# FFT and feed-forward on one core: the folds of w_in's second to fourth quarter from float32r halves

## The chip, the cores and the metric

The kernel runs on one core of a Trainium2 chip. The metric is the device time of one launch in microseconds (us). The kernel before takes 1676.99 us, the median of three runs (1676.96 to 1677.31).

A core has a matrix engine (TensorE, PE in the profile; its weight loads are PEld), VectorE (DVE), ScalarE (ACT), GpSimd (POOL) and SyncE (SP), which issues DMAs. Each engine takes its instructions in its own order and waits, where it must, for a count of another engine's finished instructions.

## The reference

`x` has 8 x 3008 rows of 256. A Fourier transform over both axes is taken and its real part kept; the result goes through a feed-forward layer of width 2048:

```
X = np.fft.fft(np.fft.fft(x, axis=1), axis=2).real     # (8, 3008, 256)
h = X.reshape(24064, 256) @ w_in                       # (24064, 2048)
g = np.where(h >= 1, h, np.where(h <= -1, 0, (h + 1) ** 2 / 4))
out = g @ w_out                                        # (24064, 256)
```

`w_in` and `w_out` come as float64 and are made float32 by the kernel itself.

## The kernel before

The transform over 256 columns is not taken for itself: its cosine and sine matrices (`mats`, two of 256 x 128, as four 128 x 128 tiles in `cm`) are multiplied into `w_in` once. This is the fold. It is done by quarters f4 of 512 columns, for the cosine (m = 0) and the sine (m = 1): fold n = 2 f4 + m, n = 0 to 7. A fold is two float32 matmuls into one PSUM bank `wps` (`fold_half`, one for each 128 rows of `w_in`). `fold_w_in` has ScalarE write the bank's high half to `wh`, rounded to float32r, and `fold_low` (s) has VectorE write what is left to `wl`. From fold 3, 5 and 7 ScalarE takes a row as well (R, `take_delta`), which four small DMAs (r, `move_delta`) spread to `delta`.

The main loop runs over units: 48 per batch element, one for each chunk of up to 512 columns and each block of 128 of the 2048. A unit i has on TensorE six float32r matmuls into two banks uv (`gemm1`: `wh` and `wl` with the high and low half of the transform), on VectorE a step us and two steps h, on ScalarE two steps a, on VectorE a step g, and on TensorE the acc matmuls (`gemm2`), some units later. The first 20 units take g as float32 and do four float32 acc matmuls; later ones take halves and do twelve in float32r. Three PSUM banks serve uv, and folds 3 and 5 take one of them as well. `SKIP` leaves units 7 and 11 without acc matmuls.

While the first units run, the weights are still being converted. Job n = 0, 1, 4, 5, 8, 9, 12, 13 is a half (128 rows) of a quarter of `w_in`, the others are parts of `w_out`. A conversion takes VectorE for two field steps (A, B or a), ScalarE (b), VectorE for one or two joins (c), and GpSimd for the products (d), whose result is `f32s[n]`, the tile `cv_n` in the profile. These tiles share a few buffers (tags h, a, gl), each of which goes round.

What runs when is written out by hand, in strings of one letter and a number per step: `START`, and for each unit `AHEAD` (between us and h on VectorE), `AMID` (after h), and `STEPS` (before `|`: ahead of the acc matmuls, after it: behind them). Up to unit 23 the engines' orders are pinned to the order of writing. Steps named `Q`, `W`, `M` and the like are put `behind_vector`: GpSimd starts them when VectorE's last instruction written before them is done.

In units 7 to 17 there lie the folds of quarters two to four: before, folds 2 and 3 between uv 7 and uv 8, folds 4 and 5 between uv 11 and uv 12, fold 6 behind the acc block of unit 15 and fold 7 before that of unit 17.

Of the kernel before, what the change touches and what calls it, by code (L numbers as in the profile page):

```python
# [9 lines left out]
F32 = mybir.dt.float32  # L10
F32R = mybir.dt.float32r
U32 = mybir.dt.uint32
I16 = mybir.dt.int16
AF = mybir.ActivationFunctionType
ALU = mybir.AluOpType
# [6 lines left out]
NB, S, D, FF = 8, 3008, 256, 2048  # L22
NA, NBB, NC = 64, 47, 24
P = 128
# [5 lines left out]
CH = 512  # L30
NCHUNK = 3
NFT = FF // P
ZPAD = 40
# [6 lines left out]
SHIFT = [23, 7, 7]  # L40
# [5 lines left out]
def _constants():  # L46
# [36 lines left out]
)  # L83
AHEAD = {1: "p12 v2 G0 q11", 2: "b3", 3: "p13 d3", 5: "L1", 6: "u1 d4", 7: "e14", 8: "M R1", 11: "d6", 12: "r2 M", 14: "s4", 15: "d7 e11", 17: "M u2", 18: "d10 M", 21: "M", 22: "u6 Q4", 23: "Q5", 30: "M M", 32: "M"}
AMID = {0: "p11 b2", 1: "h E1 q12", 4: "q13", 5: "p14", 6: "q14 A9", 7: "f2 B9 a8", 8: "b9 c8", 9: "c6", 11: "M a7 f4", 12: "b7", 16: "O1", 17: "a15 a14 f7", 18: "b14 b15", 19: "Q2 s7", 21: "c15", 22: "M", 25: "M M"}
STEPS = {
    0: "c2 | D1",
    1: "L0 e5",
# [2 lines left out]
    4: "b5 | L3 c4",  # L91
    5: "e6 | c5",
    6: "a12 d5",
    7: "b8 | b12 M s2 f3",
    8: "s3 d8 | a6 b6 e13",
    9: "r1 | c9 M",
    10: "u0 | d9 M L2",
    11: "f5 A13 R2",
    12: "c12 l11 B13 b13",
    13: "c13 d13 d12 | a10 s5",  # L100
    14: "e10 e7 b10 | c7",
    15: "M Q0 | f6 M",
    16: "s6 A11 B11",
    17: "R3 c10 | b11 e15 u3",
# [29 lines left out]
SPARE = (3, 5)  # L134
# [6 lines left out]
def fft_ffn_kernel(ctx: ExitStack, tc: tile.TileContext, x, xn, cst, w_in, w_out, out):  # L141
    nc = tc.nc

    wts = ctx.enter_context(tc.tile_pool(name="wts", bufs=1))
    sb = ctx.enter_context(tc.tile_pool(name="sb", bufs=1))
    dr = ctx.enter_context(tc.tile_pool(name="dr", bufs=1, space=bass.MemoryType.DRAM))
    ps = ctx.enter_context(tc.tile_pool(name="ps", bufs=1, space=bass.MemoryType.PSUM))
# [65 lines left out]
    cm = sb.tile([P, _OFF[6] - _OFF[2]], F32, tag="nyb", name="cm", bufs=4)  # L213
# [13 lines left out]
    def fft_bank(b, name):  # L227

        if name in BANK:
            return ps.tile([P, CH], F32, tag=BANK[name], name=name, bufs=1)  # L230
        if b == 0 and early[0] < EARLY_BANKS:
            early[0] += 1
            return ps.tile([P, CH], F32, tag=f"acc{early[0] % 4}", name=name, bufs=1)
        return ps.tile([P, CH], F32, tag="fft", name=name, bufs=1)
# [9 lines left out]
    raws, f32s, wo32, shared = {}, {}, {}, {}  # L244
# [95 lines left out]
    def behind_vector(ins):  # L340
        last = [ins for ins in traced if ins.engine == mybir.EngineType.DVE][-1]
        tc.add_manual_dep(ins, last.name, data_sync, reason="beside VectorE's next steps")

    folds, deltas, spreads = {}, {}, {}
# [21 lines left out]
    def fold_half(n, h):  # L366
        f4, m = divmod(n, 2)
        if h == 0:
            if f4 == 0 or n in SPARE:
                folds[n] = ps.tile([P, CH], F32, tag="uv", name=f"wps_{n}", bufs=3)  # L370
            else:
                folds[n] = fft_bank(f4, f"wps_{n}")
        nc.tensor.matmul(folds[n], mats[m][h], f32s[4 * f4 + h], start=(h == 0), stop=(h == 1))  # L373

    def fold_w_in(n):
        f4, m = divmod(n, 2)
        cols = slice(f4 * CH, (f4 + 1) * CH)
        if n not in folds:
            fold_half(n, 0)
        fold_half(n, 1)  # L380
        nc.scalar.activation(wh[m][:, cols], folds[n], AF.Copy, scale=inner if m else 1.0)

    def take_delta(f4):
# [14 lines left out]
    s1, s2, zn = {}, {}, {}  # L398
# [183 lines left out]
    def signs(i):  # L582
        return (slice(0, 1), slice(1, 2)) if i == n_units - 1 else (slice(0, 2),)

    def gemm1(i):
# [11 lines left out]
        nc.vector.scalar_tensor_tensor(us, nyb[b, k][:, :n], delta[:, f : f + 1], uv[0], op0=ALU.mult, op1=ALU.add)  # L597
        run_steps(AHEAD.get(i, ""))
        h = sb.tile([P, 2, CH], F32, tag="h", name=f"h_{i}", bufs=4)[:, :, :n]
# [3 lines left out]

        run_steps(AMID.get(i, ""))
        for sg in signs(i):
# [114 lines left out]
    def piece_sums(n):  # L720
# [31 lines left out]
        "v": lambda n: convert_scale(n, nc.vector),  # L752
        "F": lambda n: fold_half(n, 0),
        "f": fold_w_in,
        "G": activate,
        "s": fold_low,
        "u": w_out_high,
        "O": w_out_low,
        "Q": lambda n: behind_vector(w_out_low(n, nc.gpsimd)),
# [8 lines left out]
    def run_steps(names):  # L768
        for s in names.split():
            steps[s[0]](int(s[1:] or 0))  # L770
# [17 lines left out]
    for i in range(n_units + LAG):  # L788
# [29 lines left out]
        if i < n_units:  # L818
            run_steps(then)
            change = units[i][2] == (FIRST if b == 0 else 0) + LAG  # L820
            while pending and (change or units[i][2] != (FIRST if b == 0 else 0) + LAG - 1 and done < total * (r + 1 - r0) / (per - r0)):
                change = False
                w, f = pending.pop(0)
                f()
                done += w
                n = XC if b + 1 < PLAIN else XT
# [92 lines left out]
```

## Time and profile before

| | |
|---|---|
| median of three runs | 1676.99 us |
| the profiled execution | 1677.08 us |
| its span, first to last instruction | 1675.3 us |
| TensorE busy | 1669.6 us (100%) |
| VectorE, ScalarE, GpSimd busy | 81%, 79%, 71% of the span |
| granted TensorE clock | 1.000 |

A busy TensorE is one that has a matmul in flight: matmuls are pipelined, a record of 0.39 us stands for one that follows the last by 0.23 us, and a float32 matmul makes two records. The chain of waits gives TensorE's time without that overlap. Times of the rows are from the start of the span.

### The profile page before, as it was taken

To read this page: it belongs to the slowest core of one execution; us is meant where nothing else is said; L and a number is where in the kernel's file an instruction comes from. 1 tells how busy PE (TensorE), PEld (TensorE's weight loads), DVE (VectorE), ACT (ScalarE), POOL (GpSimd) and SP (SyncE) were. 2 spreads that over 40 slices of the span, in tenths; PEclk is the share of its full clock that TensorE was granted. 3 is DMA by queue.
4 is the path that set the end of the run, shared out by engine and by line. 5 is a ranking of instruction groups with operands and counts; after the bars stand their busy time and mean duration, and the time that the engine had idled before them with its cause. 6 is when DMAs were issued, how large, how long until landed. Compare 5 with 4: busy or idle time off the path is not lost.

```text
span 1675.3 us, 21422 instructions
## 1 busy us (share of the span) xinstructions
PE 1669.6 (100%) x7722; PEld 1382.0 (82%) x7722; DVE 1364.4 (81%) x1743; ACT 1327.8 (79%) x1527; POOL 1185.7 (71%) x957
## 2 busy tenths in 40 slices
PE   9999999999999999999999999999999999999999
PEld 6557888888888888888888888888888888888887
DVE  8998899877887787877887778787787777788776
ACT  6778878877888777887788877888778887778786
POOL 2447869856987568976789657896588866566664
PEclk9999999999999999999999999999999999999999
DMA  9113111100011000110010100101001010000000
GB/s 351 49 51 117 57 63 58 62 14 32 26 45 62 20 26 26 57 49 20 26 59 24 54 15 26 63 20 62 18 15 63 1 37 32 1 26 22 3 25 26
DMA packets 35705, 75.49 MB, mean 45 GB/s; under 512 B 4624, under 2 KB 13840, under 8 KB 35600
## 3 DMA queue, kind: packets, MB, share of 16 engines
q1 hardware_dynamic: 35420, 74.00, 12.5%
q8 instruction: 60, 0.98, 0.2%
q14 instruction: 45, 0.37, 0.1%
q10 hardware_dynamic: 180, 0.14, 0.0%
HBM read 46.31 MB, written 27.81 MB: 44 GB/s over the span
## 4 chain that ended last, share of the span: by engine, by line
PE 99%; DVE 1%; DMA 0%; issue 0%; SPq 0%; ACT 0%; DVEq 0%
PE acc L680 62%; PE uv L594 30%; PE s L549 2%; PE s L419 2%; PE wps L373 1%; PE s L424 0%; DMA raw<-in_moe_w_in_dram 0%; DVE us L597 0%; DVE h L600 0%; DVE h L601 0%; PE ny L523 0%; DVE g L620 0%; DVE pql L238 0%; DVE cv L304 0%; DVE cv L303 0%
## 5 line engine op out<-in xcount | busy, mean ns | idle before, releaser
L643 POOL TENSOR_TENSOR gl<-h,gh 128x512 fp32r<-128x512 f32 (+1 forms) x724 | 911.0, 1281 | 379.0 <-PE acc L680 207.4
L606 ACT ACTIVATE a<-h,biases 128x1024 f32<-128x1024 f32 (+1 forms) x385 | 436.0, 1133 | 242.5 <-DVE h L601 240.4
L680 PE MATMUL acc<-gh,woh 128*128 128x512 f32 (+1 forms) x1456 | 566.9, 389 | 0.0
L680 PE MATMUL acc<-gh,wol 128*128 128x512 f32 (+1 forms) x1456 | 558.8, 384 | 0.0
L680 PE MATMUL acc<-gl,woh 128*128 128x512 f32 (+1 forms) x1456 | 558.3, 383 | 0.0
L624 DVE SCALAR_TENSOR_TENSOR h<-a,h 128x1024 f32<-128x1024 f32 (+1 forms) x365 | 492.0, 1348 | 2.3 <-ACT a L607 1.0
L597 DVE SCALAR_TENSOR_TENSOR us<-nyb,delta,uv 128x512 f32<-128x512 f32 (+1 forms) x384 | 282.4, 735 | 243.8 <-PE uv L594 243.3
L627 ACT ACTIVATE gh<-h 128x1024 fp32r<-128x1024 f32 (+1 forms) x365 | 380.8, 1043 | 52.4 <-DVE h L624 38.1
L607 ACT ACTIVATE a<-a 128x1024 f32<-128x1024 f32 (+1 forms) x385 | 394.9, 1026 | 1.1
L680 PEld LDWEIGHTS acc<-gl,woh 128*128 128x128 f32 x1456 | 272.5, 187 | 52.0
L680 PEld LDWEIGHTS acc<-gh,woh 128*128 128x128 f32 x1456 | 273.0, 187 | 48.7
L680 PEld LDWEIGHTS acc<-gh,wol 128*128 128x128 f32 x1456 | 272.8, 187 | 48.6 <-DVE wol L335 0.3
L594 PE MATMUL uv<-pqh,wh 128*128 128x512 f32 (+1 forms) x768 | 303.2, 395 | 0.0
L600 DVE TENSOR_TENSOR h<-us,uv 128x512 f32<-128x512 f32 (+1 forms) x384 | 260.0, 677 | 51.1 <-POOL gl L643 0.8
L594 PE MATMUL uv<-pqh,wl 128*128 128x512 f32 (+1 forms) x768 | 294.3, 383 | 0.0
L594 PE MATMUL uv<-pql,wh 128*128 128x512 f32 (+1 forms) x768 | 294.3, 383 | 0.0
L601 DVE TENSOR_TENSOR h<-us,uv 128x512 f32<-128x512 f32 (+1 forms) x384 | 257.2, 670 | 0.0
L594 PEld LDWEIGHTS uv<-pqh,wh 128*128 128x128 f32 x768 | 143.8, 187 | 31.2 <-issue 3.8
L594 PEld LDWEIGHTS uv<-pqh,wl 128*128 128x128 f32 x768 | 143.7, 187 | 31.1 <-issue 5.0
L594 PEld LDWEIGHTS uv<-pql,wh 128*128 128x128 f32 x768 | 143.7, 187 | 27.6 <-DVE pql L238 0.4
L184 POOL TENSOR_TENSOR x<-x 120x256 f32<-120x256 f32 x84 | 96.5, 1149 | 13.7 <-DVE h L624 6.1
L189 POOL TENSOR_TENSOR x<-x 120x256 f32<-120x256 f32 (+1 forms) x49 | 65.7, 1341 | 11.1 <-DVE h L624 7.0
(85 smaller groups left out, 804.9 us busy)
## 6 DMA issues: line engine op xcount, KB each, us to landing
x<-in_xn_dram SPq DMA_DIRECT2D x42, 512.0 KB, 3.4
out_dram<-o SPq DMA_DIRECT2D x26, 512.0 KB, 2.7
out_dram<-o SPq DMA_DIRECT2D x14, 482.0 KB, 2.8
nyb<-nyr SPq DMA_DIRECT2D x24, 256.0 KB, 3.3
x<-in_x_dram SPq DMA_DIRECT2D x8, 512.0 KB, 7.3
raw<-in_moe_w_in_dram SPq DMA_DIRECT2D x4, 512.0 KB
raw<-in_moe_w_out_dram SPq DMA_DIRECT2D x4, 512.0 KB, 9.2
part<-o SPq DMA_DIRECT2D x4, 512.0 KB
```

The lines of the kernel that those rows point to most:

```text
L184: return nc.gpsimd.tensor_tensor(t[:, r], t[:, r], t[:, r + 1], op=ALU.add).ins
L189: return nc.gpsimd.tensor_tensor(t[:, 1], t[:, 0], t[:, 2], op=ALU.add).ins
L594: nc.tensor.matmul(t[:, :n], w[m][:, cols], r[:, m], start=(j == 0), stop=(j == 2))
L597: nc.vector.scalar_tensor_tensor(us, nyb[b, k][:, :n], delta[:, f : f + 1], uv[0], op0=ALU.mult, op1=ALU.add)
L600: nc.vector.tensor_tensor(h[:, 0], us, uv[1], op=ALU.subtract)
L601: last_h = nc.vector.tensor_tensor(h[:, 1], us, uv[1], op=ALU.add).ins
L606: nc.scalar.activation(a[:, sg], h[:, sg], AF.Relu, bias=half, scale=0.5)
L607: nc.scalar.activation(a[:, sg], a[:, sg], AF.Square)
L624: g = nc.vector.scalar_tensor_tensor(h[:, sg], a[:, sg], 1.0, h[:, sg], op0=ALU.min, op1=ALU.max).ins
L627: nc.scalar.activation(gh[:, sg], h[:, sg], AF.Copy)
L643: ins = nc.gpsimd.tensor_tensor(gl[:, sg], h[:, sg], gh[:, sg].bitcast(F32), op=ALU.subtract).ins
L680: nc.tensor.matmul(acc[:, :n], w, g[:, sg], start=(begin and j == 0), stop=(last and j == len(terms) - 1))
```

## The change

The folds of the second to fourth quarter (n = 2 to 7) take float32r. One new step S (`halve_mats`) has ScalarE copy the four matrix tiles to float32r (`hi`, 128 x 512) and GpSimd subtract that from them (`lo`). For each half quarter a step H (`halve_high`) has ScalarE copy `f32s[n]` to float32r and a step W (`halve_low`) has GpSimd subtract. All go to one tile `halved`, in the buffer of z, with room for one quarter. The fold is then six matmuls: high with high, matrix low with weight high, matrix high with weight low, each for two blocks of 128 rows. The two folds of the first quarter stay.

The strings move folds 2, 3, 4 and 5 behind the acc matmuls of units 8, 9, 12 and 13, with their low halves, rows and delta DMAs after them.

```
-AHEAD = {... 7: "e14", 8: "M R1", 11: "d6", 12: "r2 M", 14: "s4", ...}
+AHEAD = {... 7: "e14 S", 8: "M", 11: "d6", 12: "M", ...}
-AMID = {... 7: "f2 B9 a8", ... 11: "M a7 f4", ...}
+AMID = {... 7: "B9 a8", ... 11: "M a7", ...}
-    7: "b8 | b12 M s2 f3",
-    8: "s3 d8 | a6 b6 e13",
-    9: "r1 | c9 M",
-    10: "u0 | d9 M L2",
-    11: "f5 A13 R2",
-    12: "c12 l11 B13 b13",
-    13: "c13 d13 d12 | a10 s5",
-    14: "e10 e7 b10 | c7",
+    7: "H4 H5 W4 W5 b8 | b12 M",
+    8: "d8 | f2 a6 b6 e13",
+    9: "s2 | f3 R1 c9 M",
+    10: "s3 u0 | r1 d9 H8 W8 M L2",
+    11: "H9 W9 A13",
+    12: "c12 l11 f4 B13 b13",
+    13: "c13 d13 d12 s4 | f5 R2 a10",
+    14: "s5 H12 H13 W12 W13 e10 e7 b10 | r2 c7",
...
+        nc.scalar.activation(hi, cm, AF.Copy)
+        nc.gpsimd.tensor_tensor(lo, cm, hi.bitcast(F32), op=ALU.subtract)
+
+    def halve_high(n):
+        nc.scalar.activation(halved["w", 0, n % 2], f32s[n], AF.Copy)
+
+    def halve_low(n):
+        hi, lo = (halved["w", i, n % 2] for i in range(2))
+        behind_vector(nc.gpsimd.tensor_tensor(lo, f32s[n], hi.bitcast(F32), op=ALU.subtract).ins)
+
+    def fold_in_halves(n):
+        f4, m = divmod(n, 2)
+        if n in SPARE:
+            folds[n] = ps.tile([P, CH], F32, tag="uv", name=f"wps_{n}", bufs=3)
+        else:
+            folds[n] = fft_bank(f4, f"wps_{n}")
+        terms = [(i, j, h) for i, j in ((0, 0), (1, 0), (0, 1)) for h in range(2)]
+        for at, (i, j, h) in enumerate(terms):
+            w = halved["m", i][:, (2 * m + h) * P : (2 * m + h + 1) * P]
+            nc.tensor.matmul(folds[n], w, halved["w", j, h], start=(at == 0), stop=(at == len(terms) - 1))
```

On TensorE, before, behind unit 7's last uv matmuls (`uv_1_531`) and up to unit 8's (`uv_0_565`):

```order
L594 MATMUL uv_1_531<-pql_1_298,wh_69 128x512
L373 MATMUL wps_542<-cv_410,cm 128x512
L373 MATMUL wps_542<-cv_415,cm 128x512
L373 MATMUL wps_561<-cv_410,cm 128x512
L373 MATMUL wps_561<-cv_415,cm 128x512
L594 MATMUL uv_0_565<-pqh_2_389,wh_68 128x512
```

and now, from the same place to the fold, behind unit 8's uv (`uv_0_563`, `uv_1_567`) and an acc block:

```order
L629 MATMUL uv_1_531<-pql_1_298,wh_69 128x512
L629 MATMUL uv_0_563<-pqh_2_389,wh_68 128x512
...
L629 MATMUL uv_1_567<-pql_2_390,wh_69 128x512
L715 MATMUL acc_0_514<-g_512,wo_330 128x512
L715 MATMUL acc_1_515<-g_512,wo_330 128x512
L715 MATMUL acc_2_516<-g_512,wo_330 128x512
L715 MATMUL acc_3_517<-g_512,wo_330 128x512
L405 MATMUL wps_592<-halved 128x512 x6
```

The uv matmuls of units 7 and 8 now follow each other, and the fold stands one unit later.

On ScalarE now, between unit 10's last eviction and unit 12's first step (`a_702` is unit 11, `a_729` unit 12, `cv_546` and `cv_508` are the halves of the third quarter, n = 8 and 9):

```order
L731 ACTIVATE o_1_670<-acc_3_517 128x512
L390 ACTIVATE halved<-cv_546 128x512
L641 ACTIVATE a_702<-h_699,biases 128x1024
L642 ACTIVATE a_702<-a_702 128x1024
L390 ACTIVATE halved<-cv_508 128x512
L289 ACTIVATE cv_704<-cv_704 128x512
L290 ACTIVATE cv_704<-cv_704,biases 128x512
L292 ACTIVATE raw_wol<-raw_wol 128x512
L641 ACTIVATE a_729<-h_726,biases 128x2x482
```

Before, fold 4's eviction stood where the first copy to `halved` stands, and nothing where the second does.

On GpSimd now, from the product of `cv_508` to the second subtraction of that quarter (x are steps of the next batch element's input, `wo_697` a part of `w_out`):

```order
L320 TENSOR_TENSOR cv_508<-cv_508 128x512
L394 TENSOR_TENSOR halved<-cv_546,halved 128x512
L184 TENSOR_TENSOR x_1_458<-x_1_458 120x256
L320 TENSOR_TENSOR wo_697<-cv_600 128x512
L189 TENSOR_TENSOR x_1_458<-x_1_458 120x256
L394 TENSOR_TENSOR halved<-cv_508,halved 128x512
```

The three steps between stood there before as well; the subtractions are new ahead of them and behind them.

## Rows read from the trace of the kernel before

**Rows 1.** The page's engines: busy us (share of the span) x instructions.

```profile
PE 1669.6 (100%) x7722; PEld 1382.0 (82%) x7722; DVE 1364.4 (81%) x1743; ACT 1327.8 (79%) x1527; POOL 1185.7 (71%) x957
```

**Rows 2.** TensorE's waits, whole run: us in total, times, longest us.

```profile
PE warm_bank L713 <- POOL warm L708: 1.3, 1, 1.3
PE wps L373 <- DVE cv L320: 0.3, 1, 0.3
```

**Rows 3.** One stretch: us, busy PE, PEld, DVE, ACT, POOL; clock, DMA share, GB/s.

```profile
44.00:120.00 76.00, 76.00 (x234) 43.16 (x233) 74.09 (x109) 59.44 (x78) 33.23 (x32) 1.00 0.16 55
```

**Rows 4.** The chain of waits, 40 to 130 us: start us, us, what.

```profile
55.80 3.43 PE wps L373 x8
...
60.60 3.43 PE acc L680 x8
...
83.14 1.29 PE uv L594 x6
...
97.31 1.72 PE wps L373 x4
```

**Rows 5.** Timeline of VectorE: start us, us, engine, line, what.

```profile
55.85 0.73 DVE L597 SCALAR_TENSOR_TENSOR us<-nyb,delta,uv 128x512 f32<-128x512 f32 x1
...
60.04 0.71 DVE L396 TENSOR_TENSOR wl<-wps,wh 128x512 fp32r<-128x512 f32 x1
60.64 0.76 DVE L597 SCALAR_TENSOR_TENSOR us<-nyb,delta,uv 128x512 f32<-128x512 f32 x1
...
72.42 0.74 DVE L597 SCALAR_TENSOR_TENSOR us<-nyb,delta,uv 128x512 f32<-128x512 f32 x1
...
80.00 0.43 DVE L271 TENSOR_SCALAR cv<-raw 128x512 uint32<-128x512 uint32 x1
80.34 0.72 DVE L597 SCALAR_TENSOR_TENSOR us<-nyb,delta,uv 128x482 f32<-128x482 f32 x1
...
89.58 1.49 DVE L276 TENSOR_SCALAR cv<-raw 128x512 uint32<-128x512 uint32 x1
...
91.66 0.70 DVE L597 SCALAR_TENSOR_TENSOR us<-nyb,delta,uv 128x482 f32<-128x482 f32 x1
```

**Rows 6.** Timeline of ScalarE.

```profile
60.19 0.62 ACT L289 ACTIVATE cv<-cv 128x512 f32<-128x512 uint32 x1
...
74.59 1.15 ACT L606 ACTIVATE a<-h,biases 128x1024 f32<-128x1024 f32 x1 [3.35 <-DVE h L601]
...
76.73 0.61 ACT L331 ACTIVATE woh<-wo 128x512 fp32r<-128x512 f32 x1
...
79.64 1.18 ACT L606 ACTIVATE a<-h,biases 128x1024 f32<-128x1024 f32 x1
...
81.81 0.67 ACT L381 ACTIVATE wh<-wps,biases 128x512 fp32r<-128x512 f32 x1
```

**Rows 7.** GpSimd's groups, 44 to 120 us: busy us, mean ns, idle before.

```profile
L320 POOL TENSOR_TENSOR wo<-cv 128x512 f32<-128x512 f32 x4 | 5.1, 1286 | 8.8 <-DVE cv L304 4.5 <-ACT cv L289 4.2
L184 POOL TENSOR_TENSOR x<-x 120x256 f32<-120x256 f32 x5 | 3.7, 737 | 6.6 <-DVE cv L304 5.2 <-DVE g L620 1.4
...
L335 POOL TENSOR_TENSOR wol<-wo,woh 128x512 fp32r<-128x512 f32 x2 | 2.6, 1284 | 0.0
```

**Rows 8.** Timelines of VectorE and GpSimd where they meet.

```profile
97.28 1.59 POOL L297 TENSOR_SCALAR raw<-raw 128x512 f32<-128x512 uint32 x1
97.64 1.30 DVE L620 SCALAR_TENSOR_TENSOR g<-a,h 128x964 f32<-128x964 f32 x1
...
112.39 1.28 POOL L311 TENSOR_TENSOR cv<-cv,raw 128x512 f32<-128x512 f32 x1
112.46 2.23 DVE L620 SCALAR_TENSOR_TENSOR g<-a,h 128x964 f32<-128x964 f32 x1
```

**Rows 9.** SyncE's timeline, quarter two's delta DMAs; their line's time to landing.

```profile
63.31 2.46 SPq L362 DMA_DIRECT2D delta<-row  x4
DMA to landing us min/median/max: 2.0/2.0/2.8
```

More of the change, by code (lines that the diff above doesn't have):

```diff
@@ L83 @@
 )
-AHEAD = {1: "p12 v2 G0 q11", 2: "b3", 3: "p13 d3", 5: "L1", 6: "u1 d4", 7: "e14", 8: "M R1", 11: "d6", 12: "r2 M", 14: "s4", 15: "d7 e11", 17: "M u2", 18: "d10 M", 21: "M", 22: "u6 Q4", 23: "Q5", 30: "M M", 32: "M"}
-AMID = {0: "p11 b2", 1: "h E1 q12", 4: "q13", 5: "p14", 6: "q14 A9", 7: "f2 B9 a8", 8: "b9 c8", 9: "c6", 11: "M a7 f4", 12: "b7", 16: "O1", 17: "a15 a14 f7", 18: "b14 b15", 19: "Q2 s7", 21: "c15", 22: "M", 25: "M M"}
+AHEAD = {1: "p12 v2 G0 q11", 2: "b3", 3: "p13 d3", 5: "L1", 6: "u1 d4", 7: "e14 S", 8: "M", 11: "d6", 12: "M", 15: "d7 e11", 17: "M u2", 18: "d10 M", 21: "M", 22: "u6 Q4", 23: "Q5", 30: "M M", 32: "M"}
+AMID = {0: "p11 b2", 1: "h E1 q12", 4: "q13", 5: "p14", 6: "q14 A9", 7: "B9 a8", 8: "b9 c8", 9: "c6", 11: "M a7", 12: "b7", 16: "O1", 17: "a15 a14 f7", 18: "b14 b15", 19: "Q2 s7", 21: "c15", 22: "M", 25: "M M"}
 STEPS = {
@@ L373, in fold_half, with halve_mats @@
         nc.tensor.matmul(folds[n], mats[m][h], f32s[4 * f4 + h], start=(h == 0), stop=(h == 1))
+    halved = {}
+    def halve_mats():
+        t = sb.tile([P, ZPAD + NC * (P + 1)], F32R, tag="z", name="halved", bufs=1)
+        wide = 4 * P
+        for i in range(2):
+            halved["m", i] = t[:, i * wide : (i + 1) * wide]
+            for h in range(2):
+                o = 2 * wide + SHIFT[1] + (2 * i + h) * CH
+                halved["w", i, h] = t[:, o : o + CH]
+        hi, lo = (halved["m", i] for i in range(2))
+        nc.scalar.activation(hi, cm, AF.Copy)
[15 more added lines that the diff above has]
+            nc.tensor.matmul(folds[n], w, halved["w", j, h], start=(at == 0), stop=(at == len(terms) - 1))
     def fold_w_in(n):
@@ L377, in fold_w_in @@
         cols = slice(f4 * CH, (f4 + 1) * CH)
-        if n not in folds:
-            fold_half(n, 0)
-        fold_half(n, 1)
+        if f4:
+            fold_in_halves(n)
+        else:
+            if n not in folds:
+                fold_half(n, 0)
+            fold_half(n, 1)
         nc.scalar.activation(wh[m][:, cols], folds[n], AF.Copy, scale=inner if m else 1.0)
@@ L756, in fft_ffn_kernel @@
         "s": fold_low,
+        "S": lambda n: halve_mats(),
+        "H": halve_high,
+        "W": halve_low,
         "u": w_out_high,
```

## The prediction

> **What bounds the kernel now.** I read the page's table of engines first, then TensorE's waits, then the stage in which the change lies. TensorE is busy for 1669.6 of 1675.3 us [rows 1], and over the whole run its records show two waits, 1.6 us together, both in the first 9 us [rows 2]. Whatever is taken from TensorE, or makes it wait, therefore reaches the end one to one. The chain of waits in the stage from 40 to 130 us says the same: it runs through TensorE alone, units of six uv matmuls (1.37 us, the gap between the end of the fold block at 59.23 and the acc block at 60.60) and of four acc matmuls (3.43 us) [rows 4].
>
> But that stage has a second limit. From 44 to 120 us VectorE is busy for 74.1 of 76 us [rows 3]: it converts the weights beside its share of each unit. Its first step of unit 10 starts at 72.42 us [rows 5], 2.9 us after TensorE had the data (60.60 + 3.43 + 1.37 + 3.43 + 0.68 = 69.5 [rows 4]). TensorE does not notice, since a PSUM bank of uv is wanted again only one unit later. So the reader is to see a stage with TensorE full and VectorE full, the second a few us behind the first, and every queue in its written order. A wait put in front of VectorE here can't be made up before about 100 us.
>
> **The change part by part.**
>
> *The folds on TensorE.* Before, the second and third quarter's folds are two blocks of 3.43 us and the fourth quarter's two of 1.72 us [rows 4]: 10.3 us. A fold in halves is six float32r matmuls of 512 columns, which is what one unit's uv matmuls are: 1.37 us, six folds 8.2 us. Gain 2.1 us. [...]
>
> *Unit 8 directly behind unit 7.* The folds leave the place between uv 7 and uv 8, which has no acc block either. The second half of uv 8 takes the bank of uv 7's first, so it needs VectorE's us step of unit 7, 55.85 to 56.58 [rows 5]; TensorE is ready for it at 55.80 + 0.68 = 56.48. With 0.2 us for signal and start (an estimate, used below too): 0.3 us lost.
>
> *Fold 2's halves.* ScalarE reaches the two copies of `cv_4`, `cv_5` when unit 7's square is through, at 60.19, where its next instruction started before [rows 6]; a copy takes 0.61 us. GpSimd then subtracts twice, 1.28 us each [rows 7]: 60.85 to 63.4. TensorE wants the last of its six matmuls at 55.80 + 0.3 + 1.37 + 3.43 + 1.14 = 62.0, so it waits 1.6 us, or 2.2 if VectorE's two joins of `cv_8`, due in those us, get between the subtractions. This wait is not in the sum by itself: a later one, below, sets TensorE's time anew.
>
> *VectorE from unit 8 to 10.* The two low halves of quarter two (0.60 us each, from 60.04 to 60.64 [rows 5]) move: one out from before unit 8, one in before unit 10. Unit 8's step then starts at 60.04, unit 10's 72.42 - 60.64 = 11.78 us later, at 71.8. What is new there are GpSimd's subtractions of 1.28 us, beside VectorE's work. The rows show that some pairs don't run together: a field step of VectorE took 1.49 us instead of 0.43, started 0.1 us into a GpSimd instruction [rows 5], and a g step 2.23 beside GpSimd's add at 112.39 [rows 8]. So the two subtractions cost VectorE between 0 and 2 x 1.28 = 2.6 us. I take 1.6: one hit in full and a smaller one. [...]
>
> *The chain to fold 4 — the term that decides.* Let T be the start of ScalarE's first step of unit 10. It follows unit 10's us step by 74.59 - 72.42 = 2.17 us [rows 5, 6]: T is 74.0 without new hits, 75.6 with 1.6 us of them, 76.6 at most. From T, ScalarE does unit 10's two steps, woh, four evictions and one more copy before unit 11's first step, 79.64 - 74.59 = 5.05 us; the copy of `cv_8` (H8) takes the slot of the fold's eviction there. H8 is done at T + 5.2. Unit 11's two steps take 81.81 - 79.64 = 2.17 us, and only then stands the copy of `cv_9` (H9), done at T + 7.8. GpSimd has between its subtractions W8 and W9 two x steps (0.74) and a wo product (1.29) [rows 7]: W8 from T + 5.2 to 6.5, the three to T + 9.2, W9 to T + 10.5. GpSimd, not H9, is last.
>
> Two things wait for W9. Fold 4's sixth matmul does: TensorE starts uv 13 at T + 10.5 + 0.2 + 0.2 = T + 10.9 = 86.5, where before it started at 83.14 with fold 5 already done [rows 4]. And VectorE does: the first field step of `cv_13` (A13) takes the buffer of `cv_9`, whose last reader was fold 5 on TensorE and is now W9. It was at 80.00, directly before unit 12's us step at 80.34 [rows 5]; now it starts at T + 10.6 and unit 12 at T + 10.9 = 86.5, so VectorE, full until then, stands some 5 us. Behind it wait units 12 and 13 and the conversion of quarter four.
>
> *Behind that.* TensorE: uv 13 with 0.25 for its second bank, acc, fold 5 (1.37), uv 14 (1.29), acc: T + 22.0. VectorE needs 91.66 - 80.34 = 11.3 us from unit 12's to unit 14's us step [rows 5], with one low half (0.6) in either order, and 1.07 us of a hit inside. Until fold 5's low half is taken only two uv banks go round, so uv 15's first half waits for unit 14's us step, done at T + 23.0, and its second for unit 14's last h step, 2.1 us after the us step began, T + 24.4. The second half of uv 15 starts at T + 24.6 = 100.2. Before: 97.31 - 3.43 - 0.65 = 93.2 [rows 4]. TensorE is 6.9 us late. Folds 6 and 7 give back 0.35 each, fold 6 waits about 0.2 for its second subtraction.
>
> *The rest.* The four small delta DMAs of quarter two now stand on SP behind two part stores, which wait for the four evictions (T + 4.6): at 0.6 us an issue (2.46/4) the first is issued about T + 5.8 = 81.4 and landed 2.0 later [rows 9], 83.4. Unit 12 needs it at 86.5, so the A13 wait covers it; without that wait it would be what is late next, 3 us against the old 80.34. The tile of the halves uses z's buffer, wanted again only in unit 24: nothing. The extra 7 copies (0.61) and 7 subtractions (1.28) fit, ScalarE and GpSimd being busy for 59 and 33 of the 76 us [rows 3]; their places cost, not their sum. After 120 us nothing is done that would let TensorE catch up.
>
> **Sum.** 6.9 - 0.7 + 0.2 = 6.4 us later. The profiled execution took 1677.08 us, 1.8 around its span, and the median is 1676.99, the same within the runs' spread; 1677.0 + 6.4 = 1683.4.
>
> **Rivals.**
> 1. No new hits: T is 74.0 and the hit of 1.07 falls away, uv 15's second half at 97.5, +4.3 - 0.5: 1680.8. For it: GpSimd's subtractions are told to stand behind a VectorE step, whose next ones read PSUM. Against: the joins of `cv_8` come inside 2.6 us.
> 2. More hits: T = 76.6 and another 1.28 between units 12 and 14: +9.3 - 0.5, 1685.8. [...]
> 3. The other side: W9 is done before TensorE wants it, all halves are hidden, the 2.1 us remain: 1674.9. TensorE without waits wants fold 4's last matmul at 80.5 (six uv or folds of 1.37, four acc blocks, 1.29, 1.14 and 0.3 behind 55.80), so it decides whether T + 10.5 is below that: T would have to be 70.0, 4 us before its lowest value. Only a shorter way of ScalarE and GpSimd than the rows have would give it.
> 4. [...]
> 5. The change doesn't do what it says: six float32r matmuls, each with a new weight load, take no less than the float32 fold. +2.1 on the forecast: 1685.5. Against: the uv matmuls change weights each time too.
>
> **How the numbers follow.** Forecast 0.50, rivals 0.18, 0.18, 0.07, 0.04, 0.03. I take 0.2% (3.35 us) as what a measurement of this kernel tells from no change: slower is above 1680.35, faster below 1673.65. The forecast, rivals 2, 4, 5 and 0.10 of rival 1 lie above: 0.85. The rest of 1 and most of 3: 0.13. No case reaches faster; 0.02 for what I don't see. The range from 1679.9 to 1686.5 holds all but rivals 3 and 4 and the tails.
>
> **What the profile of the changed kernel would show.** The fold's rows as float32r, six of about 0.23 us each. A wait of 1.5 to 2.2 us on TensorE in fold 2, on GpSimd's halves; one of 1 us or more in fold 4, the same; VectorE idle for about 5 us before a field step near 86 us, released by GpSimd; uv 13 at 85 to 87.5 us; from 120 us on the same picture as before, 4 to 9 us later. If uv 13 starts before 83.5, or VectorE's pause isn't there, the chain to W9 is wrong; if uv 13 is right and uv 16 isn't 6 us late, the hits are mis-sized.

## The result and the profile after

The changed kernel takes 1686.11 us (median of 6 runs, 1685.51 to 1687.2), the kernel before 1676.97 (6 runs, 1676.86 to 1677.31): a ratio of 1.0055, with a 95% interval of 1.0044 to 1.0065. It is 9.1 us slower. The forecast was 1683.4, 6.4 us slower, with a range of 1679.9 to 1686.5: the direction and the place are right, the size is 2.7 us too small.

The page's engines come first, beside [rows 1]: TensorE has two more us of work in its records and GpSimd 12 more; the span is 9.0 us longer, 1684.3 instead of 1675.3.

```profile
PE 1671.7 (99%) x7734; PEld 1383.0 (82%) x7734; DVE 1369.3 (81%) x1743; ACT 1332.1 (79%) x1534; POOL 1198.1 (71%) x964
```

Then TensorE's waits over the whole run (us in total, times, longest us), where [rows 2] had two:

```profile
PE wps L405 <- POOL halved L394: 2.8, 2, 1.5
PE uv L629 <- DVE us L632: 1.9, 3, 1.5
...
PE uv L629 <- DVE h L636: 0.8, 2, 0.4
PE uv L629 <- DVE wl L429: 0.8, 1, 0.8
PE wps L405 <- ACT halved L390: 0.7, 1, 0.7
```

All of them lie between 56 and 103 us. TensorE now waits for GpSimd's halves in the folds, and for VectorE in the uv blocks. VectorE has two waits of its own between 44 and 130 us:

```profile
DVE cv L271 <- POOL halved L394: 5.0, 1, 5.0
DVE cv L303 <- POOL cv L287: 1.8, 1, 1.8
```

The first is the pause before A13, as forecast. The second, a join of `cv_6` that waits for GpSimd, was not in the forecast. The stretch of [rows 3] again shows both engines with holes, where both were full:

```profile
44.00:120.00 76.00, 68.89 (x218) 38.93 (x217) 67.78 (x96) 54.20 (x74) 38.69 (x33) 1.00 0.15 55
```

VectorE's timeline, beside [rows 5] (start us, us, engine, line, what; in brackets the idle time before it and its releaser):

```profile
62.47 1.75 DVE L304 SCALAR_TENSOR_TENSOR cv<-raw_wol,cv 128x512 uint32<-128x512 uint32 x1
64.15 1.63 DVE L655 SCALAR_TENSOR_TENSOR g<-a,h 128x1024 f32<-128x1024 f32 x1
...
70.47 0.69 DVE L303 SCALAR_TENSOR_TENSOR cv<-raw_wol,cv 128x512 f32<-128x512 uint32 x1 [1.85 <-POOL cv L287]
...
74.62 0.74 DVE L632 SCALAR_TENSOR_TENSOR us<-nyb,delta,uv 128x512 f32<-128x512 f32 x1
...
87.42 0.43 DVE L271 TENSOR_SCALAR cv<-raw 128x512 uint32<-128x512 uint32 x1 [5.01 <-POOL halved L394]
87.76 0.71 DVE L632 SCALAR_TENSOR_TENSOR us<-nyb,delta,uv 128x482 f32<-128x482 f32 x1
...
97.23 1.19 DVE L271 TENSOR_SCALAR cv<-raw 128x512 uint32<-128x512 uint32 x1
98.34 1.49 DVE L276 TENSOR_SCALAR cv<-raw 128x512 uint32<-128x512 uint32 x1
99.75 0.70 DVE L632 SCALAR_TENSOR_TENSOR us<-nyb,delta,uv 128x482 f32<-128x482 f32 x1
```

The reader is to see three places. The join at 62.47 takes 1.75 us instead of 0.68, and the g step behind it 1.63 instead of 1.22. The join at 70.47 stands still for 1.85 us. So unit 10's us step starts at 74.62, 2.8 us behind the 71.8 that the moved low halves alone would give. And A13 starts at 87.42, unit 12 at 87.76, 7.4 us later than the 80.34 of before.

GpSimd's timeline over the same us says why:

```profile
60.63 3.05 POOL L394 TENSOR_TENSOR halved<-cv,halved 128x512 fp32r<-128x512 f32 x2 [3.77 <-DVE us L632]
63.76 0.94 POOL L287 TENSOR_SCALAR cv<-cv 128x512 f32<-128x512 uint32 x1
64.78 1.93 POOL L201 TENSOR_SCALAR x<-x 24x128 f32<-24x128 f32 x1
...
69.82 0.62 POOL L287 TENSOR_SCALAR cv<-cv 128x512 f32<-128x512 uint32 x1
...
82.09 1.44 POOL L394 TENSOR_TENSOR halved<-cv,halved 128x512 fp32r<-128x512 f32 x1 [5.33 <-ACT halved L390]
...
86.12 1.26 POOL L394 TENSOR_TENSOR halved<-cv,halved 128x512 fp32r<-128x512 f32 x1
```

The second of `cv_8`'s two joins lies beside W5, and each side is slowed: the join takes 1.75 us, the pair of subtractions (60.63 to 63.68) 3.05 us instead of 2 x 1.28. Behind them stand GpSimd's small jobs: the mantissa of `cv_12` at 63.76, four x steps, a product, and at 69.82 the mantissa of `cv_6`, for which VectorE then waits. The first x step, at 64.78, is slowed as well: beside VectorE's g step and the two field steps behind it, it takes 1.93 us, where before it took 0.52:

```profile
60.23 0.52 POOL L201 TENSOR_SCALAR x<-x 24x128 f32<-24x128 f32 x1 [3.83 <-DVE g L620]
```

So the queue grew by more than the subtractions themselves. W9, at 86.12 to 87.38, releases A13. Last, ScalarE's part of that chain, beside [rows 6], and TensorE's places behind it, beside [rows 4]:

```profile
76.79 1.15 ACT L641 ACTIVATE a<-h,biases 128x1024 f32<-128x1024 f32 x1 [4.78 <-DVE h L636]
...
81.36 0.65 ACT L390 ACTIVATE halved<-cv 128x512 fp32r<-128x512 f32 x1
...
84.05 0.61 ACT L390 ACTIVATE halved<-cv 128x512 fp32r<-128x512 f32 x1
```

```profile
63.73 0.50 PE L405 MATMUL wps<-halved 128*128 128x512 f32 x1 [1.26 <-POOL halved L394]
...
87.44 0.50 PE L405 MATMUL wps<-halved 128*128 128x512 f32 x1 [1.54 <-POOL halved L394]
...
100.51 0.49 PE L629 MATMUL uv<-pqh,wh 128*128 128x482 f32 x1 [1.52 <-DVE us L632]
...
101.83 0.49 PE L629 MATMUL uv<-pqh,wh 128*128 128x482 f32 x1 [0.41 <-DVE h L636]
```

### The profile page after: what moved, and what is told of

Same layout as the page of the kernel before. It is cut to its first block, busy times and chain, and to the rows that moved or that the text cites. A ratio compares the mean times of both kernels' runs of the same rounds, so it can differ in the third digit from the quotient of the medians.

```text
span 1684.3 us, 21460 instructions
## 1 busy us (share of the span) xinstructions
PE 1671.7 (99%) x7734; PEld 1383.0 (82%) x7734; DVE 1369.3 (81%) x1743; ACT 1332.1 (79%) x1534; POOL 1198.1 (71%) x964
## 2 busy tenths in 40 slices
DMA packets 35706, 75.51 MB, mean 45 GB/s; under 512 B 4624, under 2 KB 13840, under 8 KB 35600
## 4 chain that ended last, share of the span: by engine, by line
PE 92%; DVE 5%; POOL 1%; issue 1%; ACT 0%; DMA 0%; SPq 0%; DVEq 0%; POOLq 0%; ACTq 0%
PE acc L715 58%; PE uv L629 29%; PE s L454 2%; PE s L584 2%; DVE g L655 1%; DVE us L632 1%; DVE h L636 1%; DVE h L635 1%; DVE cv L304 0%; PE s L459 0%; DVE cv L276 0%; POOL halved L394 0%; DVE cv L271 0%; DMA raw<-in_moe_w_in_dram 0%; DVE cv L303 0%
## 5 line engine op out<-in xcount | busy, mean ns | idle before, releaser
L184 POOL TENSOR_TENSOR x<-x 120x256 f32<-120x256 f32 x84 | 95.0, 1131 | 11.3 <-DVE h L659 5.8
L488 ACT ACTIVATE z<-s 64x240 f32<-64x240 f32 (+1 forms) x196 | 69.2, 353 | 4.4 <-PE s L454 1.0
```

The lines of the kernel that those rows point to most:

```text
L184: return nc.gpsimd.tensor_tensor(t[:, r], t[:, r], t[:, r + 1], op=ALU.add).ins
L488: nc.scalar.activation(z[to, :, at : at + n], src[:, :, t0 : t0 + n], AF.Copy)
```

## The experiments

Four theories were put against each other. H: GpSimd's subtractions and a full VectorE hold each other up. P: the chain of copies and subtractions to W9, and with it VectorE's pause before A13, is the loss. W: TensorE's own waits on the halves are the loss. M: the new order of the folds is. Times are differences of medians to the kernel before in the same set of runs (1677.02, 1677.09 and 1677.16 us); the changed kernel stands at +9.1.

**The pause taken away.**

```
-    11: "H9 W9 A13",
-    12: "c12 l11 f4 B13 b13",
+    11: "H9 W9",
+    12: "c12 l11 A13 f4 B13 b13",
```

> The field step of cv_13 (A13), which waits for GpSimd's W9, is moved behind unit 12's us, h and g steps of VectorE; all else as in the changed kernel (1686.1 us, 9.1 over the kernel before). Theory P, the pause: VectorE's 5.0 us of idle time at 82.4 to 87.4 us are the loss. Then unit 12's us step starts when its deltas have landed, about 83.5 to 84.5 us instead of 87.76, and 3 to 4 us come back: 1682.5 (+5.5). Theory H, the collisions: VectorE is full and loses its time beside GpSimd's subtractions; the pause was only where the lateness showed, and with VectorE at work W9 (1.26 us) now stands behind its two-input steps, so TensorE waits about 3 us in fold 4 instead of 1.5 and uv 13 starts at 87 to 90 us in spite of it: 1684 to 1685.5 (+7 to +8.5). Theory M, the moved folds alone: no change, 1686.

Measured: 1684.37 us, +7.35, ratio 1.0043 (1.0029 to 1.0058). VectorE doesn't pause for W9 any more, but unit 12's us step starts at 85.28, not when unit 11's g step is through, at 82.2 (80.92 + 1.24):

```profile
85.28 0.72 DVE L632 SCALAR_TENSOR_TENSOR us<-nyb,delta,uv 128x482 f32<-128x482 f32 x1 [3.11 <-DMA delta<-row]
```

The four delta DMAs, now behind two part stores, are what is late next, as the prediction said. So a wait of 5.0 us has become one of 3.1: unit 12's us step comes 2.5 us earlier than in the changed kernel, unit 14's 1.7 (98.09 instead of 99.75), and 1.7 us came back. The +7.35 lies where H had it, but not by H's way, since TensorE waits 1.57 us in fold 4 and not 3. This run takes away less than the pause, and doesn't tell H from P. The granted clock is 0.62 from 88 to 92 us, unit 13's uv matmuls there start 0.40 us apart instead of 0.21, and what that costs isn't split off.

**The subtractions taken away.** W4 to W13 are not issued; the kernel leaves the weights' low halves out, and TensorE reads the high ones again.

```
-            nc.tensor.matmul(folds[n], w, halved["w", j, h], start=(at == 0), ...
+            nc.tensor.matmul(folds[n], w, halved["w", 0, h], start=(at == 0), ...
-    7: "H4 H5 W4 W5 b8 | b12 M",
+    7: "H4 H5 b8 | b12 M",
-    10: "s3 u0 | r1 d9 H8 W8 M L2",
-    11: "H9 W9 A13",
+    10: "s3 u0 | r1 d9 H8 M L2",
+    11: "H9 A13",
-    14: "s5 H12 H13 W12 W13 e10 e7 b10 | r2 c7",
+    14: "s5 H12 H13 e10 e7 b10 | r2 c7",
```

> The changed kernel without GpSimd's six subtractions W4 to W13 (the low halves of the weights are left out: the third pair of products of a fold reads the high halves instead, so TensorE does the same six matmuls). ScalarE's copies and the order stay. Theory P: fold 4 and A13 then wait for H9, 7.8 us behind ScalarE's first step of unit 10 instead of W9's 10.5, so the pause is about 2 us instead of 5 and some 3 us come back: 1683. Theory H: the 1.85 us wait of the join of cv_6 and the long joins and g steps at 62 to 67 and 97 to 114 us go as well, unit 10's us step starts at 72 instead of 74.62 us, and in all 5 us come back: 1681 (+4). Theory M: nothing comes back, 1686. What is left over the kernel before is the price of the order and of the copies.

Measured: 1681.03 us, +4.0, ratio 1.0026 (1.0015 to 1.0037). VectorE's timeline has the join at its short time again and a shorter pause:

```profile
63.02 0.68 DVE L304 SCALAR_TENSOR_TENSOR cv<-raw_wol,cv 128x512 uint32<-128x512 uint32 x1
...
82.76 0.43 DVE L271 TENSOR_SCALAR cv<-raw 128x512 uint32<-128x512 uint32 x1 [1.75 <-ACT halved L390]
```

So six instructions of GpSimd, 7.7 us of its time (6 x 1.28), cost 5.1 of the 9.1 us, as H had it. The part of the pause that W9 makes is in these 5.1.

**The subtractions done, but not read.** Of the edits above only the first, in `fold_in_halves`; W4 to W13 stay. The weights' low halves are made and left out of the folds.

> The changed kernel with all subtractions done, but no fold reads them: the third pair of products reads the high halves again (the low halves of the weights are left out of the sum). TensorE then never waits for W4 to W13; GpSimd, ScalarE and VectorE do what they did, and A13 still waits for W9. Theory W, TensorE's own waits: the waits on GpSimd's halves (1.26 and 1.54 us, with smaller ones some 3.5 us) come back: 1682.6. Theories P and H: TensorE only arrives earlier and waits for VectorE's us steps instead, since VectorE's steps start no earlier: 1685.5 to 1686.5.

Measured: 1686.08 us, +9.06, ratio 1.0055 (1.0040 to 1.0070). TensorE's waits between 40 and 140 us moved from the folds to the uv blocks:

```profile
PE uv L629 <- DVE us L632: 3.7, 3, 1.8
PE uv L629 <- DVE h L636: 0.9, 2, 0.4
```

Theory W falls: the 2.8 us on GpSimd's halves are gone, and nothing came back. The clock doesn't hide a gain here. The profiled run has it at 0.61 from 88 to 92 us, but TensorE is at uv 15 at 100.65 all the same, and uv 15's second half, at 101.98 (101.83 in the changed kernel), waits for VectorE's h step. TensorE is not what is late; VectorE is.

**The new order with float32 folds.** `fold_w_in` takes float32 halves for all quarters, no S, H or W; since folds 4 and 5 read the float32 weights, the steps of `cv_13` stand behind fold 5.

```
...
-    13: "c13 d13 d12 s4 | f5 R2 a10",
+    13: "d12 s4 | f5 R2 A13 B13 b13 a10",
-    14: "s5 H12 H13 W12 W13 e10 e7 b10 | r2 c7",
+    14: "s5 c13 d13 e10 e7 b10 | r2 c7",
```

> The new order of the folds with float32 folds: no copies, no subtractions, no split matrices. Since folds 4 and 5 read the float32 weights, cv_13's field steps stand behind fold 5 and its join behind them. Theory M, the moved folds are the loss: 1684 or more. Theories P and H: what the halves bring in is gone, and what is left is the price of folds that no longer fill the places between uv 7 and uv 8 and between uv 11 and uv 12, with a full VectorE, and of cv_13 made later: 2 to 4 us, 1679 to 1681. If the order is free: 1677.

Measured: 1682.36 us, +5.3, ratio 1.0032 (1.0019 to 1.0045). More than H and P expected, less than M. Moving `cv_13` is a change of its own here, and VectorE's waits have a part that no halves explain:

```profile
DVE us L632 <- DMA delta<-row: 3.1, 2, 2.3
```

So the order has a price, but this run can't say which; the last but one below gives it together with ScalarE's copies.

**The halves beside the kernel before.** Its folds stay float32 and in their places; S, H and W of the changed kernel stand beside them, and nothing reads them.

```
-    7: "b8 | b12 M s2 f3",
+    7: "H4 H5 W4 W5 b8 | b12 M s2 f3",
-    10: "u0 | d9 M L2",
-    11: "f5 A13 R2",
+    10: "u0 | d9 H8 W8 M L2",
+    11: "H9 W9 f5 A13 R2",
-    14: "e10 e7 b10 | c7",
+    14: "H12 H13 W12 W13 e10 e7 b10 | c7",
```

> The kernel before, its float32 folds where they were, and beside them the split of the matrices, the seven copies and the seven subtractions at the changed kernel's places; nothing reads them. TensorE's work is that of the kernel before to the instruction. A13 waits for W9 here too, since both use cv_9's buffer. Theory H (GpSimd's subtractions cost a full VectorE its time, and the chain of copies and subtractions holds VectorE in front of A13): nearly the whole loss is there without any change on TensorE, 1683 to 1687 (+6 to +10), with a pause of 5 us before A13. Theory M (the order of the folds, or the float32r folds themselves): the copies and subtractions fit beside the rest, 1677 to 1679.

Measured: 1685.41 us, +8.3, ratio 1.005 (1.0035 to 1.0065). VectorE's timeline:

```profile
62.59 1.25 DVE L304 SCALAR_TENSOR_TENSOR cv<-raw_wol,cv 128x512 f32<-128x512 uint32 x1
63.77 1.09 DVE L305 SCALAR_TENSOR_TENSOR cv<-raw_wol,cv 128x512 uint32<-128x512 uint32 x1
...
86.11 0.43 DVE L272 TENSOR_SCALAR cv<-raw 128x512 uint32<-128x512 uint32 x1 [5.46 <-POOL halved L395]
```

With not one matmul changed, making the halves costs nearly as much as the whole change: the long joins and the pause are both here. A part of it is TensorE's clock, though. It waited 3.8 us for unit 12's us step, and then the granted clock was 0.50 from 88 to 92 us, over uv 13 and into the acc block behind it (one stretch, columns as in [rows 3]; the clock is the third number from the end):

```profile
88.00:92.00 4.00, 4.00 (x8) 2.30 (x8) 3.90 (x7) 3.43 (x4) 0.00 (x0) 0.50 0.00 0
```

From uv 13's start to uv 14's TensorE took 7.3 us (87.22 to 94.50), before 4.7 (82.58 to 87.30). How much of these 2.6 us reaches the end isn't split from the rest.

**The copies beside the kernel before.** The same without W4 to W13.

> The kernel before with ScalarE's seven copies and the split of the matrices beside it, but without the six subtractions of the weights; nothing reads what is made. It differs from the run with all halves beside the kernel before (+8.3 us) by the subtractions alone. A13 now waits for H9 instead of W9. If the subtractions are the dear part (theory H): a pause of about 3 instead of 5.5 us before A13 and no long joins at 62 to 66 us, 1680 to 1681.5 (+3 to +4.5). If the chain of ScalarE's copies is the dear part (theory P): A13's pause shortens by what W9 took after H9, 2.7 us, and no more, 1682.7. If the copies are free: 1677.

Measured: 1680.26 us, +3.1, ratio 1.0017 (1.0008 to 1.0027). VectorE's pause before A13 is 2.9 us, on ScalarE's H9. The difference between the two runs, 5.2 us, is the price of the subtractions a second time, in another order and with float32 folds (with the clock's part in it). The chain of copies by itself costs 3.1.

**H9 and W9 a unit earlier.**

```
-    10: "s3 u0 | r1 d9 H8 W8 M L2",
-    11: "H9 W9 A13",
+    10: "s3 u0 | r1 d9 H8 H9 W8 W9 M L2",
+    11: "A13",
```

> The changed kernel with H9 and W9 moved one unit forward, directly behind H8 and W8. By the trace of the changed kernel H8 starts at 81.36 us; H9 follows at 82, W9 is done at about 84.7 instead of 87.38, A13 starts then, the pause is 2.4 us instead of 5.0. Theory P (the chain to W9 decides): the 2.6 us come back in full, 1683.5. Theory H (collisions): W9 and the product of cv_6 now meet other steps of VectorE, and VectorE needs its us steps of units 13 and 14 for uv 15 as before: 1 to 1.5 us come back, 1684.6 to 1685.1.

Measured: 1684.97 us, +7.9, ratio 1.0046 (1.0031 to 1.0061). The pause is 2.4 instead of 5.0 us, and by the medians 1.2 came back of these 2.6. But the four runs lie from 1683.96 to 1685.6, and the profiled one is the lowest (+6.9, so 2.3 came back), with unit 14's us step at 97.59, 2.2 us earlier, and a granted clock of 1.00 in the whole stage. So the median speaks for H and the profiled run nearly for P; this part of the pause came back almost whole where the clock stayed up.

**Pause and delta wait both gone.** As the run before, with `A13` behind unit 12's steps and `r1` directly behind `R1`, ahead of the part stores.

```
-    9: "s2 | f3 R1 c9 M",
-    10: "s3 u0 | r1 d9 H8 H9 W8 W9 M L2",
-    11: "A13",
-    12: "c12 l11 f4 B13 b13",
+    9: "s2 | f3 R1 r1 c9 M",
+    10: "s3 u0 | d9 H8 H9 W8 W9 M L2",
+    11: "",
+    12: "c12 l11 A13 f4 B13 b13",
```

> As the run before with H9 and W9 forward, and with A13 behind unit 12's steps and the four delta DMAs ahead of the two part stores on SP: neither W9 nor the deltas (the 3.1 us wait that took the pause's place when A13 alone was moved) stand before unit 12's us step. It should start about 82.3 us, directly behind unit 11's g. Theory P: both waits of VectorE are gone, uv 13 starts at about 84.5 and the loss is the 3 to 4 us that VectorE had lost before unit 10: 1680.5 to 1681.5. Theory H: VectorE gets no less to do and meets the subtractions and products of GpSimd elsewhere; it loses on the way to unit 14's us step what it gained: 1684 to 1685.

Measured: 1684.53 us, +7.4, ratio 1.0043 (1.0029 to 1.0058). Unit 12's us step starts at 82.15 us, 5.6 earlier than in the changed kernel, but unit 14's at 97.52, only 2.2 earlier. In between, VectorE's and GpSimd's timelines:

```profile
85.68 1.24 DVE L303 SCALAR_TENSOR_TENSOR cv<-raw,cv 128x512 f32<-128x512 uint32 x1
86.84 1.75 DVE L304 SCALAR_TENSOR_TENSOR cv<-raw,cv 128x512 uint32<-128x512 uint32 x1
88.52 0.94 DVE L271 TENSOR_SCALAR cv<-raw 128x512 uint32<-128x512 uint32 x1
```

```profile
84.58 1.79 POOL L184 TENSOR_TENSOR x<-x 120x256 f32<-120x256 f32 x1
86.32 1.72 POOL L320 TENSOR_TENSOR wo<-cv 128x512 f32<-128x512 f32 x1
```

In the changed kernel the same joins took 0.68 and 0.69 us (at 90.85 and 91.46), because GpSimd had worked through its queue during the pause. Here both sides are slow, and most of what the pause had cost is paid in collisions (A13, which now stands between, and a wait of 0.54 us for a subtraction make the rest). That is where 3.4 of theory P's 5.6 us went. The other 2.2 are there at uv 15 (second half at 99.61 instead of 101.83), but then the granted clock of the profiled run is 0.60 from 100 to 102 us and 0.55 from 102 to 104, and five of the acc block's eight records take 4.00 us, in the changed kernel all eight 3.59. The four runs are 1683.51 and 1684.02, with a mean clock of 1.000, and 1685.03 (the profiled one) and 1685.26 with 0.999. In the first two, +6.4 and +6.9, 2.2 to 2.7 us came back.

**GpSimd copies with one input in place of the subtractions.**

```
-    nc.gpsimd.tensor_tensor(lo, f32s[n], hi.bitcast(F32), op=ALU.subtract)
+    nc.gpsimd.tensor_scalar(lo, f32s[n], 1.0, None, op0=ALU.mult)
```

> The changed kernel with GpSimd's six subtractions of the weights replaced by GpSimd copies with one input (times 1.0, so the low halves are left out and the third pair of products is of no use); they take about 0.66 instead of 1.28 us. All waits stay. If what VectorE loses is that its two-input steps stand still beside a two-input GpSimd instruction, joins, h and g steps run through beside these (as g did at 97.64 us in the kernel before), only the field steps meet them, and the chain is shorter by 0.6 us at each: some 2.5 us back, 1683.5. If any GpSimd instruction that reads SBUF stops VectorE, in proportion to its length: half of what the subtractions cost (5.1 us by the run without them), also about 1683.5, but then joins and g beside the copies show it, at 62 to 66 us. If the number of instructions counts: 1686.

Measured: 1682.77 us, +5.7, ratio 1.0037 (1.0024 to 1.0049). 3.4 us came back, more than the 2.5 expected, and not for the reason given: such a copy takes 1.49 us, longer than a subtraction alone (1.29); 0.66 us is what GpSimd's mantissa step takes on a 128x512 tile (at 55.74 us in the kernel before). The joins of VectorE beside it are short:

```profile
60.16 2.94 POOL L394 TENSOR_SCALAR halved<-cv 128x512 fp32r<-128x512 f32 x2 [3.17 <-DVE g L655]
```

```profile
62.03 0.73 DVE L303 SCALAR_TENSOR_TENSOR cv<-raw_wol,cv 128x512 f32<-128x512 uint32 x1
62.69 0.68 DVE L304 SCALAR_TENSOR_TENSOR cv<-raw_wol,cv 128x512 uint32<-128x512 uint32 x1
```

So it is not GpSimd's busy time that stops these joins; the instruction with one SBUF input in its place lets them run. Unit 10's us step starts at 73.42, 1.2 us earlier than in the changed kernel. The edit does a second thing, though: a copy doesn't read ScalarE's high half, so it doesn't wait for it. W8 starts before ScalarE's H8 (80.17), and the pause before A13 is shorter for that too:

```profile
77.54 1.49 POOL L394 TENSOR_SCALAR halved<-cv 128x512 fp32r<-128x512 f32 x1 [1.97 <-DVE wl L429]
```

```profile
84.82 0.43 DVE L271 TENSOR_SCALAR cv<-raw 128x512 uint32<-128x512 uint32 x1 [1.69 <-POOL halved L394]
```

How the 3.4 us divide between the two isn't shown.

**No subtractions, no pause, no delta wait.** The second run's edits, with `A13` behind unit 12 and `r1` ahead of the part stores.

> The changed kernel without the six subtractions (low halves of the weights left out), with A13 behind unit 12's steps and the delta DMAs ahead of the part stores: no collision with halves, no pause, no wait for deltas. Without subtractions alone it was 4.0 us over the kernel before, with a pause of 1.75 us and a wait of 0.41 for the deltas. Theory H with the pause as a smaller part: these 2 us come back, 1679 (+2), and what remains is the order of the folds and the waits for ScalarE's copy H9 and for the low half of fold 3. If the pause had no price of its own: 1681. If the halves were all of the loss: 1675, the 2.1 us of the folds gained.

Measured: 1678.85 us, +1.7, ratio 1.0010 (1.0001 to 1.0020). TensorE's waits between 40 and 140 us are what is left:

```profile
PE uv L629 <- DVE wl L429: 0.8, 1, 0.8
PE wps L405 <- ACT halved L390: 0.7, 1, 0.7
PE uv L629 <- DVE h L636: 0.4, 1, 0.4
PE uv L629 <- DVE us L632: 0.2, 1, 0.2
```

Even with the dear instructions and the pause away, the kernel is not faster: the places between uv 7 and uv 8 and between uv 11 and uv 12, empty now, hand a full VectorE its units sooner, and TensorE waits 1.4 us for it at uv 8, uv 11 and uv 12 (the first, third and fourth row); H9 takes 0.7 of the 2.1 us that the folds gain, which these waits use up. A remainder of 1.7 us is not split further.

**Halves for the fourth quarter alone**, in the order of the kernel before.

```
+    7: "e14 S",      # AHEAD
-    14: "e10 e7 b10 | c7",
+    14: "H12 H13 W12 W13 e10 e7 b10 | c7",
```

> The order and the folds of the kernel before, with halves for the fourth quarter alone (folds 6 and 7; their copies and subtractions ahead of unit 14's e and b steps). The folds save 2 x 0.35 = 0.7 us on TensorE. If the halves are hidden there: 1676.3. Theory H: fold 6 follows directly on the product of cv_13, so its copy and subtraction (0.6 and 1.3 us, with a collision more) stand before TensorE, which waits some 2 to 2.5 us, and a g step of VectorE is stopped: 1678.5 to 1680 (+1.5 to +3).

Measured: 1678.74 us (1677.78 to 1680.67, 10 runs), +1.6, ratio 1.0012 (1.0002 to 1.0022). TensorE waits 1.65 us for the second subtraction in fold 6, and the 0.7 us of the two folds are more than used up. The ten runs fall into two groups, six from 1677.78 to 1678.76 and four from 1680.18 to 1680.67; the mean clock is 1.000 in the six and 0.999 in the four. The profiled one belongs to the upper group, and after the wait its granted clock was 0.50 from 102 to 104 us:

```profile
98.00:100.00 2.00, 0.89 (x4) 0.26 (x2) 1.96 (x2) 1.97 (x4) 2.00 (x2) 1.00 0.00 0
102.00:104.00 2.00, 2.00 (x5) 1.33 (x4) 1.23 (x2) 0.70 (x2) 1.92 (x2) 0.50 0.99 408
106.00:108.00 2.00, 2.00 (x8) 1.24 (x7) 2.00 (x3) 1.47 (x2) 2.00 (x1) 1.00 0.00 0
```

No version tried beats the kernel before.

## Why the prediction was right in direction and short in size

**What bounds the kernel** held. A wait before VectorE in this stage is not made up: TensorE starts unit 18 8.6 us late (117.84 instead of 109.26) and the run ends 9.0 later. The run in which nothing reads the subtractions shows that VectorE, and not TensorE, carries the lateness.

**The folds on TensorE.** Six float32r matmuls in 1.37 us held where a fold doesn't wait: from the acc block at 89.28 over fold 5 to uv 14 at 94.08 are 4.80 us, 3.43 of them the acc block. Rival 5 falls.

**Unit 8 directly behind unit 7** lost 0.16 us in a visible wait (0.3 forecast), **fold 2** 1.26 us (1.6 to 2.2 forecast).

**VectorE from unit 8 to 10** is the step that was mis-sized: 1.6 us of hits were taken, bounded by 2.6, and 2.8 came. The trace has 1.07 for the join at 62.47 and 0.41 for the g step at 64.15, 1.5 together, which is the term as it was meant. What was left out is that the subtractions also delay what stands behind them on GpSimd, first of all the mantissa of `cv_6`, and VectorE's join then waited 1.85 us for it. The upper bound was of VectorE's collisions only; a queue behind the added work was not in it, nor that GpSimd's jobs in that queue are slowed by VectorE in turn (1.4 us at the x step). The three come to 3.3 us. From unit 8's us step to unit 10's it is 3.0 (59.82 to 74.62, 14.80 instead of 11.78), since the field step behind g took 0.54 instead of 0.84 us; unit 8's started 0.2 us earlier than forecast, which leaves 2.8. T was 76.79 instead of 75.6 us, 1.2 late.

**The chain to fold 4** held to a tenth of a us at its end, counted from T: W9 done at T + 10.6 (10.5 forecast), A13 at T + 10.6, unit 12 at T + 11.0 (10.9), a pause of 5.01 us ("some 5"). The 0.2 us for signal and start, the author's estimate with no row behind it, held too: uv 13 starts 0.40 us behind W9's end, with one matmul of fold 4 between. At H9's place on ScalarE there stood, before, fold 5's eviction (81.81 us [rows 6]) and its row, and not nothing. What the forecast did not see is that this pause is not a loss of its own in full: with pause and delta wait gone, unit 12 came 5.6 us earlier but unit 14 only 2.2, since GpSimd's work done in the pause then collides with VectorE, and 1.7 us came back by the medians, 2.2 to 2.7 in the two runs with the higher mean clock. The delta DMAs were the next late thing, as forecast: VectorE waited 3.1 us for them in the first run.

**Behind that.** VectorE took 11.99 us from unit 12's to unit 14's us step, 11.3 forecast: two field steps are stretched (1.19 and 1.49 us), not one. uv 15's second half started at 101.83 instead of 100.2, 8.6 us behind before. Folds 6 and 7 were to give back 0.5 net and gave nothing: uv 15 to uv 18 take 17.3 us (100.51 to 117.84), before 17.2 (92.02 to 109.26). From unit 20 to 21 TensorE loses another 0.3. So 6.4 + 1.2 (T) + 0.7 - 0.3 (uv 15 came 2.1 instead of 2.4 us behind the us step) + 0.5 + 0.3 makes 8.8 of the 9.0 us measured.

**Rivals.** 1 (no hits) fell with the long join (1.75 us), though the steps that read PSUM kept their times beside the first subtraction (h 0.69 and 0.68 us at 60.66 and 61.27); 3 (all hidden) with the pause. 2, "more hits", gave 1685.8 and came nearest to the time, by T of 76.6 and a second hit between units 12 and 14; but its T was to come from VectorE's collisions, and more than half of it was a queue. That the range held the result, with 0.4 us to spare, is in part luck: its upper end was set behind rival 2, and a term that was not counted filled the room. 4, a lower clock on TensorE, had a chance of 0.04 by the author's estimate, and no run shows that term: the granted clock in the profiled run of the changed kernel is 1.00 from 44 to 120 us. In the profiled runs of five experiments it was 0.50 to 0.62 for stretches of 2 to 4 us; in one of them a unit took 7.3 instead of 4.7 us, and in the one with the two groups of runs these lie about 2 us apart.

**How the loss divides.** With the subtractions: 9.1, and 7.4 without pause and delta wait. Without them: 4.0, and 1.7. So by the medians the subtractions are 5.1 to 5.7 us, the pause with the delta wait 1.7 to 2.3, and the order with the copies 1.7 on top of the 2.1 that the float32r folds gain. The 7.4 has runs with the lower clock in it; by the other two, 6.4 and 6.9, the subtractions are 4.7 to 5.2 and the pause 2.2 to 2.7.

## What to carry to other kernels

Work moved to an idle engine is free only if nothing that it stops, and nothing queued behind it, is needed by the engine that is full: count the collisions and the queue behind as two terms. Where an engine is full, a pause on it can be borrowed time: find out what the other engines do in it before you count its removal as a gain. When you take an instruction's input away, look whether a wait goes with it. And to price a preparation, let it run beside the old kernel with nobody reading it.

## What the runs showed of the hardware

A VectorE join with two SBUF inputs took 1.75 us beside GpSimd's subtraction (62.47 in the changed kernel) and 0.68 to 0.73 beside the one-input copy in its place; the g step took 1.62 us instead of 1.22 at 63.29 in the run with the copies, with one-input GpSimd instructions beside it, so one input is not always free.

GpSimd's one-input step on a 24x128 tile took 1.93 us beside VectorE's g step and two field steps, and 0.52 before, so the slowing goes both ways.

GpSimd's copy from float32 to float32r with one input took 1.49 us at 77.54 and at 83.30, more than the subtraction's 1.29 (median of six in the changed kernel).

With halves for the fourth quarter alone, a wait of 1.65 us on TensorE was followed in the profiled run by a granted clock of 0.50 from 102 to 104 us, and the runs of that kernel lie in two groups about 2 us apart. Waits of 1.57 us (A13 moved), 1.81 us (subtractions not read) and 3.80 us (halves beside the kernel before) were followed by 0.62, 0.61 and 0.50 from 88 to 92 us, and one of 1.59 us (pause and delta wait gone) by 0.60 and 0.55 in the two halves of 100 to 104. Waits of 1.26, 1.54 and 1.52 us (the changed kernel, 1.00 from 44 to 120 us) were not followed by it, nor were one of 1.62 us (subtractions not read, at 75.51, with the next matmuls 0.23 us apart) and the idle time of the run with H9 and W9 earlier (2.0 of the 4 us from 96 to 100, with a clock of 1.00). The runs don't show what tells the ones from the others: with 1.57 and 1.59 us on one side and 1.62 on the other, it is not the length of the wait alone.
